# Ten column blocks of a gated MLP by one level of Strassen's scheme, with their weights fetched in three phases

## The chip, the cores and the metric

The kernel runs on one core of a Trainium2 chip. The metric is the time of one execution on the device in microseconds (us); lower is better. The engines are TensorE (PE for its matmuls, PEld for its weight loads), VectorE (DVE), ScalarE (ACT), GpSimd (POOL) and SyncE (SP, whose queue issues nearly all DMAs).

## What is computed

Attention over 4 batches, 8 heads, 768 tokens and 64 features per head, masked to pairs of tokens in the same hash bucket, and then a gated MLP on its output `x` (3072 tokens by 512), cut from the reference:

```python
scores = scale * np.matmul(q, k.transpose(0, 1, 3, 2))
scores = np.where(mask, scores, -1000000000.0)
attn = softmax(scores)                       # max taken off, exp, divided by the sum
x = np.matmul(attn, v)                       # laid out as 3072 tokens x 512
gate = 1.0 / (1.0 + np.exp(-(x @ w_gate)))   # 512 x 1536, float64 weights
val = x @ w_val                              # 512 x 1536
out = (gate * val @ w_out).astype(np.float32)  # 1536 x 512
```

## The kernel before

**Numbers.** Every product of the MLP is made of three matmuls: both operands are split in a high and a low part in fp32r, and low x high, high x low and high x high are added in PSUM. The weights come as 64-bit floats and are turned into 32-bit ones on DVE, ACT and POOL ("conversion": `exponent`, `shifted`, `mantissa`, `whole`, `signed`, `scaled` in `load_w`), and then split (`high`, `low`).

**Tiles.** The 1536 hidden columns are 12 blocks `j` of 128. Tokens go in units `(b, g)`: batch `b` (4), half `g` (2) of its 768 tokens, so a unit has 384. For one unit and one block, gate and value take 4 chunks of 128 input features x 3 matmuls each (`product`, L438: 24 matmuls of 384 columns), and the output takes 3 token tiles x 3 matmuls of 512 columns (`out_product`, L471: 9). I call these 33 matmuls one column. There are 96 columns.

**Stages.** The attention stage walks through 16 pairs of heads (6 score steps each, 96 in all). In it the weights of blocks `j` 0 to 9 are converted, one per 2.2 score steps from step 12 on (`W_KEY`, `W_STEP`), and those of blocks 3 to 9 are written to DRAM (`kept`). The first `J1` = 3 blocks of the first six units are computed there too (`moe_early`), and their part of the output is written to DRAM (`part`): 18 columns. When attention has ended (`switch`), its memory is given to the other weights, and `moe_late` does the rest unit by unit: all 12 blocks for the last two units, 9 for the other six, 78 columns. Blocks 10 and 11 are converted at its beginning. Here DVE multiplies the value in PSUM by the gate (`gated`, L454), ACT makes the high part, and POOL mostly the low one (L459).

**Order.** All instructions are tasks of a planner (`Plan`): each has an engine (or two to choose from), a cost, tasks it follows, and buffers that it takes and gives. The planner plays this through with its own costs and writes the fixed order of every engine's queue. An engine waits at the head of its queue; nothing overtakes.

Of the kernel before, what the change touches and what calls it, by code (L numbers as in the profile page):

```python
# [169 lines left out]
def lsh_attention_glu_kernel(ctx, tc, q, k, v, proj, w_gate, w_val, w_out, out):  # L170
# [137 lines left out]
    def load_w(key, n, j, early, last=None):  # L308
# [21 lines left out]
        def exponent():  # L330
            z["ex"] = stage().tile([P, N_EL], I32, name=f"ex{n}{j}", tag="wex", bufs=2 if last else 1)
            nc.vector.tensor_scalar(z["ex"], z["high"], 0x7FF00000, None, op0=ALU.bitwise_and)
# [4 lines left out]
        def mantissa():  # L337
            z["mf"] = stage().tile([P, N_EL], I32, name=f"mf{n}{j}", tag="wmf", bufs=2 if last else 1)
            nc.vector.tensor_scalar(
                z["mf"], z["high"], 0x000FFFFF, 0x00100000, op0=ALU.bitwise_and, op1=ALU.bitwise_or  # L340
            )
# [14 lines left out]
        def high():  # L356
            if early or last:
                z["w"] = (w1 if early else stage()).tile([P, 2, N_EL], F32R, name=f"w{n}{j}", tag=f"w{n}{j}")
                weights[n, j] = z["w"][:, 0], z["w"][:, 1]
            else:  # L360
                z["w"] = stage1.tile([P, 2, N_EL], F32R, name=f"w{n}{j}", tag="wk", bufs=stock["wk"])
            nc.scalar.copy(z["w"][:, 0], f(z["ex"]))

        def low(eng):
            eng.tensor_sub(z["w"][:, 1], f(z["ex"]), f(z["w"][:, 0]))

        def keep():
            nc.sync.dma_start(kept[n, j], f(z["w"]))

        def fetch():  # L370
            w = later["w"].tile([P, 2, N_EL], F32R, name=f"w{n}{j}", tag=f"w{n}{j}")
            weights[n, j] = w[:, 0], w[:, 1]
            nc.sync.dma_start(f(w), kept[n, j])

        a = dma(key, CROWDED if last and j == J2 else 524288, load, after=[last or score_tasks[min(int(key), 90)]], take=["raw2" if last else "raw1"])
        b1 = add(key, "dve", 440, exponent, after=[a], take=["mid2" if last else "mid1"])
# [3 lines left out]
        d = add(key, "dve", 700, signed, after=[b2, c2], give=["raw2" if last else "raw1"])  # L380
        e = add(key, "pool", 1300, lambda: scaled(nc.gpsimd), after=[d])
        h = add(key, "act", 560, high, after=[e], take=[] if early or last else ["wk"])
        made[n, j] = add(key, "pool", 1300, lambda: low(nc.gpsimd), after=[h], give=["mid2" if last else "mid1"])
        if not early and not last:
            a = dma(key, 524288, keep, after=[made[n, j]], give=["wk"])
            fetches.append(((n, j), a, fetch))
# [6 lines left out]
    in_turn = dict(x=[], ob=[])  # L393

    def load_x(u, b, g, stored):
        z = {}

        def load():
            z["xr"] = xp.tile([P, KC, GN], F32, name=f"xr{u}", tag="xr")
            cols = slice(g * GN, (g + 1) * GN)  # L400
            nc.sync.dma_start(z["xr"], xd[b][:, :, cols].rearrange("c p t -> p c t"))

        def high(c):
            if c == 0:
# [3 lines left out]
            nc.scalar.copy(z["xh"][:, c], z["xr"][:, c])

        def low(c, eng):  # L410
            eng.tensor_sub(z["xl"][:, c], z["xr"][:, c], f(z["xh"][:, c]))
# [15 lines left out]
    def product(key, u, n, j, x, prev, last, late=False, pace=None):  # L427

        z = {"bank": ["z"] if late else ["moe", "one"]}

        def part(c):
            if c == 0:
                pool, tag = (later["ps"], "z") if late else (ps, "one")
                z["acc"] = pool.tile([P, 512], F32, name=f"z{n}{j}_{u}", tag=tag)
            hi, lo = weights[n, j]
            wc = slice(c * P, (c + 1) * P)
            for i, (a, xx) in enumerate(((lo, "xh"), (hi, "xl"), (hi, "xh"))):
                nc.tensor.matmul(  # L438
                    z["acc"][:, :GN], a[:, wc], x[xx][:, c, :],
# [508 lines left out]
```

## Time and profile before

| | |
|---|---|
| time of three runs, us | 1077.53, 1076.45, 1075.06; median 1076.45 |
| profiled execution: first to last instruction | 1071.9 us |
| PE busy | 1048.6 us (98%) |
| DVE, ACT, POOL busy | 552.2, 491.8, 260.9 us |
| chain that ended last | PE 81%, DVE 7%, ACT 4%, POOL 3% |
| HBM read, written | 70.78 MB, 28.84 MB |

The time of the profiled execution outside its span isn't listed; the median of the runs lies 4.55 us above the span. Matmul spans in the profile overlap, since they are pipelined, so the pace of PE is read from starts, not from durations. "L438" is line 438 of the kernel before.

### The profile page before, as it was taken

The page shows a single profiled execution, that of the slowest core. Times are in us where ns is not written, and L with a number is a line of the kernel's source. Part 1 is how long each engine was busy: PE and PEld are TensorE (multiplying, and loading weights), DVE is VectorE, ACT ScalarE, POOL GpSimd, SP SyncE. Part 2 cuts the span into 40 slices and gives each one's busy share as a digit, 9 for nine tenths or more (in the row PEclk, how much of TensorE's full clock was granted, in tenths as well). Part 3 has the DMA queues.
Part 4 walks back from the last instruction along what each step waited for, and adds up shares of the span by engine and source line. Part 5 has one row for each costly group of instructions (what it writes and reads, how often), then busy time and mean ns, then how long its engine had stood idle before and what let it go on. Part 6 is the DMA issues. An engine that isn't in the chain of part 4 may idle for free.

```text
span 1071.9 us, 20499 instructions
## 1 busy us (share of the span) xinstructions
PE 1048.6 (98%) x8409; PEld 849.0 (79%) x8412; DVE 552.2 (52%) x1170; ACT 491.8 (46%) x890; POOL 260.9 (24%) x239
## 2 busy tenths in 40 slices
PE   8999999999999999999999999999999999999998
PEld 5666667677676677676668999999999999999997
DVE  5888889988888878768741261111020202120201
ACT  1868786858677676657652232122121212121211
POOL 0003233332424232311003262122121212121211
PEclk9999999999999999999999999999999999999999
DMA  8146464564756554732118511002020202020000
GB/s 206 48 118 162 132 191 128 166 195 132 220 181 186 168 165 132 235 93 67 56 61 334 204 60 60 1 1 89 1 89 1 89 1 89 1 89 1 31 30 30
DMA packets 110846, 113.54 MB, mean 106 GB/s; under 512 B 60320, under 2 KB 92064, under 8 KB 110752
## 3 DMA queue, kind: packets, MB, share of 16 engines
q1 hardware_dynamic: 109024, 111.83, 34.1%
q8 instruction: 66, 1.08, 0.4%
q10 hardware_dynamic: 1728, 0.40, 0.2%
q14 instruction: 28, 0.23, 0.1%
HBM read 70.78 MB, written 28.84 MB: 93 GB/s over the span
## 4 chain that ended last, share of the span: by engine, by line
PE 81%; DVE 7%; ACT 4%; POOL 3%; DMA 2%; issue 2%; SPq 0%; POOLq 0%; DVEq 0%; ACTq 0%
PE pv L819 10%; PE zv_0l L438 8%; PE zv_1l L438 7%; PE sc L740 7%; PE zg_0l L438 7%; PE zg_1l L438 7%; PE yo_0l L471 7%; PE yo_1l L471 7%; PE tp L802 5%; PE zg L438 3%; PE zv L438 3%; PE zo L471 3%; PE sc L734 3%; DVE e L750 2%; ACT e L769 2%
## 5 line engine op out<-in xcount | busy, mean ns | idle before, releaser
L769 ACT ACTIVATE e<-e,st 128x768 f32<-128x768 f32 x192 | 196.5, 1025 | 71.1 <-DVE st L762 70.7
L750 DVE TENSOR_SCALAR_CACHE_REDUCE e<-sc 128x768 f32<-128x768 f32 x192 | 177.8, 951 | 23.2 <-PE sc L740 22.3
L819 PE MATMUL pv<-ef,vr 128*64 128x384 f32 x768 | 141.2, 498 | 0.0
L454 DVE TENSOR_TENSOR gf_1l<-zv_1l,sig 128x384 f32<-128x384 f32 x39 | 21.8, 558 | 208.5 <-PE zv_1l L438 208.5
L454 DVE TENSOR_TENSOR gf_0l<-zv_0l,sig 128x384 f32<-128x384 f32 x39 | 21.7, 558 | 192.5 <-PE zv_0l L438 192.5
L802 PEld LDWEIGHTS tp<-ident,e 64*128 64x128 f32 x2304 | 85.2, 139 | 38.9 <-issue 16.3
L802 PE MATMUL tp<-ident,e 64*128 64x64 f32 x2304 | 97.5, 226 | 5.3 <-ACT ef L809 2.9
L809 DVE COPY ef<-tp 128x768 f32<-128x768 f32 x87 | 82.0, 950 | 34.8 <-PE tp L802 32.5
L819 PEld LDWEIGHTS pv<-ef,vr 128*64 128x64 f32 x768 | 48.5, 137 | 54.5 <-issue 49.5
L740 PE MATMUL sc<-kh,ql 64*128 64x384 f32 x192 | 90.3, 470 | 0.0
L740 PE MATMUL sc<-kh,qsl 64*128 64x384 f32 x192 | 90.3, 470 | 0.0
L809 ACT COPY ef<-tp 128x768 f32<-128x768 f32 x105 | 81.6, 791 | 11.5 <-PE tp L802 11.1
L438 PE MATMUL zg_0l<-xh_0l,wg 128*128 128x384 f32 x312 | 86.5, 337 | 0.0
L438 PE MATMUL zg_1l<-xh_1l,wg 128*128 128x384 f32 x312 | 86.4, 337 | 0.0
L438 PE MATMUL zv_0l<-xh_0l,wv 128*128 128x384 f32 x312 | 85.5, 334 | 0.0
L438 PE MATMUL zv_1l<-xh_1l,wv 128*128 128x384 f32 x312 | 85.5, 334 | 0.0
L459 POOL TENSOR_TENSOR gl<-gf_1l,gh 128x384 fp32r<-128x384 f32 x39 | 40.5, 1039 | 184.4 <-ACT gh L458 184.4
L829 POOL TENSOR_TENSOR xs<-xs,rb 128x384 f32<-128x384 f32 x32 | 33.2, 1039 | 199.9 <-ACT xs L826 126.9
L459 POOL TENSOR_TENSOR gl<-gf_0l,gh 128x384 fp32r<-128x384 f32 x37 | 39.2, 1059 | 155.8 <-ACT gh L458 155.7
L734 PE MATMUL sc<-kb,qb 64*128 64x384 bf16 x384 | 64.9, 331 | 9.4 <-ACT ef L809 3.3
L471 PE MATMUL yo_0l<-wo,gh 128*128 128x512 f32 x234 | 73.5, 395 | 0.0
L471 PE MATMUL yo_1l<-wo,gh 128*128 128x512 f32 x234 | 73.5, 395 | 0.0
(151 smaller groups left out, 2453.0 us busy)
## 6 DMA issues: line engine op xcount, KB each, us to landing
kr<-in_k_dram SPq DMA_DIRECT2D x64, 96.0 KB
vr<-in_v_dram SPq DMA_DIRECT2D x16, 384.0 KB
qsh<-qh SPq DMA_DIRECT2D x32, 192.0 KB
qsl<-ql SPq DMA_DIRECT2D x32, 192.0 KB
rb<-rd SPq DMA_DIRECT2D x64, 96.0 KB
xd<-xs SPq DMA_DIRECT2D x32, 192.0 KB
rawg<-in_moe_w_gate_dram SPq DMA_DIRECT2D x12, 512.0 KB
rawv<-in_moe_w_val_dram SPq DMA_DIRECT2D x12, 512.0 KB
```

The costliest lines, as they stand in the source:

```text
L438: nc.tensor.matmul(z["acc"][:, :GN], a[:, wc], x[xx][:, c, :], start=(c == 0 and i == 0), stop=(c == KC - 1 and i == 2),)
L454: nc.vector.tensor_mul(z["gf"], z["acc"][:, :GN], sig[:, j])
L459: low = lambda eng: eng.tensor_sub(gl[:, j], z["gf"], f(gh[:, j]))
L471: nc.tensor.matmul(acc, a[:, slot, ts_], w, start=(first and i == 0), stop=(last and i == 2))
L734: nc.tensor.matmul(sc[:, j, :GN], z["qb"][rows, c], z["kb"][rows, h], start=True, stop=False, tile_position=(j * D, 0),)
L740: nc.tensor.matmul(sc[:, j, :GN], q_[rows, c], z["k" + x][rows, h * GN : (h + 1) * GN], start=False, stop=(m == 2), tile_position=(j * D, 0),)
L750: nc.vector.tensor_scalar(sp(e), gz["sc", t, h][:, :, :GN], -SCALE, None, op0=ALU.mult, op1=ALU.min, accum_out=gz["st", t][:, 0, h : h + 1],)
L769: nc.scalar.activation(e, e, AF.Exp, bias=st[:, 2, h : h + 1], scale=st[:, 1, h : h + 1], accum_out=gz["su"][:, h * GT + t : h * GT + t + 1],)
L802: nc.tensor.transpose(tp[:, r, at_ : at_ + D], gz["e", t, h][rows, c * P : (c + 1) * P], ident[rows, rows], tile_position=(r * D, 0),)
L809: copy(gz["ef", c].rearrange("p (n r d) -> p r n d", r=2, d=D), gz["tp", c][:, :, :GN].rearrange("p r (n d) -> p r n d", d=D),)
L819: nc.tensor.matmul(gz["pv"][rows, :GN], z["v"][:, h, c], gz["ef", c][:, h * GN : (h + 1) * GN], start=(c == 0), stop=(c == NC - 1), tile_p ...
L829: nc.gpsimd.tensor_mul(gz["xs"], gz["xs"], gz["rb"])
```

## The change

`J1` goes from 3 to 2, so that 16 columns are done in the old way (`moe_early` now for all eight units, the last two of them after attention), and the other ten blocks go by Strassen's scheme (Winograd's form: 7 block products, 15 sums).

**Blocks.** Two hidden blocks make a set (`SETS`: (2,3) to (10,11)), two units of one batch a pair. The 2x2 blocks are: of `x`, unit by half of the 512 features; of a weight, half of the features by hidden block. Each of 7 products (`group`, `STEPS`, in the order 1, 2, 5, 6, 3, 7, 4) is 2 chunks x 3 matmuls of 384 columns, so gate or value of a set takes 42 matmuls for a pair, where 48 stood before.

**Sums of weights.** `combined` converts the two weights of a set and makes B12-B11, B22-(B12-B11), B22-B12 and so on on POOL or DVE before they are split and kept in DRAM (`t1` to `t4`). The sets (2,3), (4,5), (6,7) are done in the attention stage (24 weights are converted there, where it were 30), (8,9) and (10,11) after it (12, where it were 6).

**Sums of x.** `x_pair` loads the four blocks of a pair, makes S1 to S4 (POOL or DVE, 128x768 each), and splits seven blocks (ACT high, POOL or DVE low, 128x768 each). Each block has one buffer, free when the pair's last value group has used it.

**Sums of products.** Every product has a PSUM bank of its own (six banks). ACT copies products 1 and 5 to SBUF, DVE adds six times per group from PSUM and SBUF (L758), and POOL or DVE adds once (`both`). The gate times the value is now a product of two SBUF tiles, on POOL or DVE.

**Phases.** `PHASES`: two sets, two sets, one set. In each phase all four batches go by, `x` is loaded and split anew for each pair, the weights of the phase are fetched from DRAM, and the output's part is fetched, added (DVE) and stored. In the last phase a pair's output products (`outs`) stand behind the next pair's groups.

Core of the diff (planner costs, release of buffers and lines of like kind left out):

```diff
-    J1 = 3
-    J2 = 10
+    J1 = 2
+    QUARTERS = 3
+    SETS = [(j, j + 1) for j in range(J1, NJ, 2)]
+    PHASES = [SETS[i : i + 2] for i in range(0, len(SETS), 2)]
...
+        for name in ("a11", "a21", "a22", "a12"):
+            raw(name)
+        pieces_of("a11")
+        summing("s1", "a21", "a22", ALU.add, [])
+        pieces_of("s1")
+        summing("s2", "s1", "a11", ALU.subtract, [ready["s1"]])
+        pieces_of("s2")
+        pieces_of("a12")
+        summing("s4", "a12", "s2", ALU.subtract, [ready["a12"]])
+        pieces_of("s4")
+        summing("s3", "a11", "a21", ALU.subtract, [got["s1"]])
+        pieces_of("s3")
+        pieces_of("a22")
...
+        1: ("a11", 0, 0), 2: ("a12", 0, 1), 5: ("s1", 1, 0), 6: ("s2", 1, 1), 3: ("s4", 3, 0), 7: ("s3", 2, 0), 4: ("a22", 2, 1),
...
+            block, piece, half = STEPS[m]
+            hi, lo = pieces[js, n, piece]
+            for c in range(2):
+                wc = slice(half * HF + c * P, half * HF + (c + 1) * P)
+                for i, (a, xx) in enumerate(((lo, "h"), (hi, "l"), (hi, "h"))):
+                    nc.tensor.matmul(
+                        bank[m], a[:, wc], x[xx, block][:, c, :], start=(c == 0 and i == 0), stop=(c == 1 and i == 2),
+                    )
...
+        for m in (1, 2, 5, 6, 3, 7, 4):
+            prev = pe(m)
+            if m == 1:
+                snap(1, "m1")
+            elif m == 2:
+                plus(2, "m1", (0, 0), tag=tag)
+                finish((0, 0))
+            elif m == 5:
+                snap(5, "t")
+            elif m == 6:
+                plus(6, "m1", "u", after=[told[0, 0]], tag="sn")
...
+            elif m == 3:
+                plus(3, "t", (1, 0), tag=tag)
+                finish((1, 0))
+            elif m == 7:
+                plus(7, "t", (1, 1), give=["sn"], tag=tag, after=[told[1, 0]])
+                finish((1, 1))
+                plus(7, "u", "u", after=[told[1, 1]])
+            elif m == 4:
+                plus(4, "u", (0, 1), give=["z", "sn"], tag=tag)
+                finish((0, 1))
```

**What moves on DVE.** After attention, DVE's queue before holds the conversion of late weights, with one PSUM multiply per column between (`raw`, `mf`, `ex` are a weight's tiles, `gf` the gated value):

```order
L344 SCALAR_TENSOR_TENSOR mfo_9357<-rawo_9259,mfo_9357 128x512
L454 TENSOR_TENSOR gf_3_0l<-zv_3_0l,sig 128x384
L349 SCALAR_TENSOR_TENSOR exo_9351<-rawo_9259,exo_9351 128x512
L459 TENSOR_TENSOR gl<-gf_3_0l,gh 128x384
L332 TENSOR_SCALAR exv_9395<-rawv_9346 128x512
L339 TENSOR_SCALAR mfv_9406<-rawv_9346 128x512
```

Now, in the first pair of the first phase (`sn`, `sg`, `gf`: sums of products; `a12`, `s1`, `sc`, `ra`: blocks of the next pair's x; `yo`: output):

```order
L650 TENSOR_TENSOR a12l_1_9342<-ra_1_9030,a12h_1_9328 128x768
L758 TENSOR_TENSOR snuv_0_0_9357<-z6v_0_0_9335,snm1v_0_0_9310 128x384
L364 SCALAR_TENSOR_TENSOR exg_9312<-rawg_9255,exg_9312 128x512
L650 TENSOR_TENSOR s1l_1_9370<-sc_1_9151,s1h_1_9359 128x768
L758 TENSOR_TENSOR gf(1, 0)v_0_0_9384<-z3v_0_0_9347,sntv_0_0_9354 128x384
L642 TENSOR_TENSOR sc_1_9151<-sc_1_9151,ra_1_8962 128x768
L772 TENSOR_TENSOR gf(1, 0)v_0_0_9384<-gf(1, 0)v_0_0_9384,sg(1, 0)g_0_0_9287 128x384
L758 TENSOR_TENSOR gf(1, 1)v_0_0_9410<-z7v_0_0_9362,sntv_0_0_9354 128x384
L642 TENSOR_TENSOR ra_1_9030<-ra_1_9030,sc_1_9151 128x768
L789 TENSOR_TENSOR gl(1, 0)4_0_0_9413<-gf(1, 0)v_0_0_9384,gh(1, 0)4_0_0_9412 128x384
```

Between two adds that empty PSUM banks (L758) now stand a late weight's conversion (L364), the next pair's sums and low parts (L642, L650), and the multiply and low part that the output product waits for (L772, L789).

**What moves on PE.** Before, the output products stand between the last value product of one unit and the first gate product of the next:

```order
L438 MATMUL zv_3_0l<-xl_0l,wv_9440 128x384
L438 MATMUL zv_3_0l<-xh_0l,wv_9440 128x384
L471 MATMUL yo_3_0l<-wo_9393,gl 128x512
L471 MATMUL yo_3_0l<-wo_9393,gh 128x512 x2
L471 MATMUL yo_3_0l<-wo_9393,gl 128x512
L471 MATMUL yo_3_0l<-wo_9393,gh 128x512 x2
L471 MATMUL yo_3_0l<-wo_9393,gl 128x512
L471 MATMUL yo_3_0l<-wo_9393,gh 128x512 x2
L438 MATMUL zg_3_1l<-xh_1l,wg_1416 128x384
```

Now, at the first pair's end in the last phase (`z4v_2_0` is product 4 of the value, phase 2, batch 0):

```order
L733 MATMUL z4v_2_0_13057<-a22h_0_12777,wv_10_12613 128x384 x2
L733 MATMUL z4v_2_0_13057<-a22l_0_12796,wv_10_12613 128x384
L733 MATMUL z4v_2_0_13057<-a22h_0_12777,wv_10_12613 128x384
L733 MATMUL z1g_2_1_13069<-a11h_1_13014,wg_10_12478 128x384
L733 MATMUL z1g_2_1_13069<-a11l_1_13028,wg_10_12478 128x384
```

At this one boundary nothing stands between the last use of one pair's x blocks and the first of the next pair's; at the others it is 36 or 72 output products.

**What moves on POOL.** Before, POOL's queue after attention is low parts, about one per column:

```order
L459 TENSOR_TENSOR gl<-gf_3_0l,gh 128x384
L411 TENSOR_TENSOR xl_1l<-xr_1l,xh_1l 128x384
L459 TENSOR_TENSOR gl<-gf_3_0l,gh 128x384
L411 TENSOR_TENSOR xl_1l<-xr_1l,xh_1l 128x384
L459 TENSOR_TENSOR gl<-gf_3_1l,gh 128x384 x11
```

Now, at the same boundary as on PE above:

```order
L642 TENSOR_TENSOR sc_1_12855<-sc_1_12855,ra_1_12798 128x768
L650 TENSOR_TENSOR a22l_1_13095<-ra_1_12814,a22h_1_13076 128x768
L772 TENSOR_TENSOR gf(1, 1)v_2_0_13092<-gf(1, 1)v_2_0_13092,sg(1, 1)g_2_0_12984 128x384
L650 TENSOR_TENSOR s2l_1_13122<-sc_1_12855,s2h_1_13107 128x768
L789 TENSOR_TENSOR gl(0, 1)10_2_0_13142<-gf(0, 1)v_2_0_13120,gh(0, 1)10_2_0_13141 128x384
```

The low part of `a22`, whose buffer is the last to come free, stands ahead of that of `s2`, which PE takes fourth.

More of the change, by code (lines that the diff above doesn't have):

```diff
@@ L306, in lsh_attention_glu_kernel, with converted @@
     fetches = []
-    def load_w(key, n, j, early, last=None):
+    def converted(key, n, j, late, which, after, first):
         z = {}
-        stage = lambda: later["w"] if last else stage1
+        stage = lambda: later["w"] if late else stage1
+        raw_, token = ("raw2", "cv2") if late else ("raw1", "cv1")
         def load():
-            z["raw"] = raw = stage().tile([P, 2 * N_EL], I32, name=f"raw{n}{j}", tag="wraw", bufs=2 if last else 1)
+            z["raw"] = raw = stage().tile([P, 2 * N_EL], I32, name=f"raw{n}{j}", tag="wraw")
             if n == "o":
@@ L354, in scaled @@
             eng.tensor_mul(f(z["ex"]), f(z["mf"]), f(z["ex"]))
[L356 to L376, printed above, removed]
+        a = dma(key, 524288, load, after=after + last_load[late], take=[raw_])
+        last_load[late] = [a]
+        b1 = add(key, "dve", 440, exponent, after=[a], take=[token] if first else [])
         b2 = add(key, "act", 700, shifted, after=[b1])
@@ L379, in load_w @@
         c2 = add(key, "dve", 700, whole, after=[c1])
[L380 to L386, printed above, removed]
+        d = add(key, "dve", 700, signed, after=[b2, c2], give=[raw_])
@@ new lines, in converted, with split, high, low @@
+        return z, add(key, "pool", 1300, lambda: scaled(nc.gpsimd), after=[d])
+    def split(key, src, to, size, late, after, give, tile_of=None):
+        z = {}
+        wk = "wk2" if late else "wk1"
+        def high():
+            if tile_of is not None:
+                z["w"] = tile_of()
+            else:
+                stage = later["w"] if late else stage1
+                z["w"] = stage.tile([P, 2, size], F32R, name=f"p{to.name}", tag="wk", bufs=stock[wk])
+            nc.scalar.copy(z["w"][:, 0], src())
+        def low():
+            nc.gpsimd.tensor_sub(z["w"][:, 1], src(), f(z["w"][:, 0]))
+        part_ = size / N_EL
+        h = add(key, "act", 60 + 500 * part_, high, after=after, take=[wk] if tile_of is None else [])
+        low_ = add(key, "pool", 100 + 1200 * part_, low, after=[h], give=give)
+        if tile_of is not None:
+            return low_, low_
+        return low_, dma(key, 1024 * size, lambda: nc.sync.dma_start(to, f(z["w"])), after=[low_], give=[wk])
@@ L871, in group @@
             )
-        a = add(n - 6, either(summed), after=[prev], take=["xs"], give=["one"])
+        ends = i == len(heads) - 1 and g == NG - 1
+        a = add(n - 6, either(summed), after=[prev], take=["xs"], give=["one"] + ["moe"] * ends)
         a = add(n - 4, "pool", 1230, divided, after=[a, spread_], give=["rb"])
```

435 lines of the change are left out of this document (333 added, 102 removed).

## The prediction

> **What bounds the kernel now.** I read the page first (busy shares, the chain that ended last), then windows by stage, then the timeline inside the end stage.
>
> ```profile
> span 1071.9 us, 20499 instructions
> PE 1048.6 (98%) x8409; PEld 849.0 (79%) x8412; DVE 552.2 (52%) x1170; ACT 491.8 (46%) x890; POOL 260.9 (24%) x239
> PE 81%; DVE 7%; ACT 4%; POOL 3%; DMA 2%; issue 2%; SPq 0%; POOLq 0%; DVEq 0%; ACTq 0%
> ```
>
> PE carries the chain. The windows (columns: span, busy us and instruction count of PE, PEld, DVE, ACT, POOL, granted clock, DMA share, GB/s) show two stages. In attention all engines are loaded; after 576 us PE alone is.
>
> ```profile
> 8.00:120.00 112.00, 106.40 (x1208) 70.01 (x1209) 95.52 (x231) 76.68 (x135) 16.62 (x14) 1.00 0.51 128
> 120.00:360.00 240.00, 232.35 (x2444) 167.25 (x2444) 209.97 (x451) 175.38 (x309) 81.28 (x69) 0.99 0.58 174
> 576.00:1068.00 492.00, 490.57 (x2562) 454.94 (x2560) 91.72 (x135) 99.96 (x202) 112.59 (x102) 1.00 0.16 57
> ```
>
> PE's pace is read from starts:
>
> ```profile
> 1051.06 0.56 DVE L454 TENSOR_TENSOR gf_1l<-zv_1l,sig 128x384 f32<-128x384 f32 x1 [5.71 <-PE zv_1l L438]
> 1054.95 0.33 PE L438 MATMUL zv_1l<-xh_1l,wv 128*128 128x384 f32 x1
> 1057.03 0.39 PE L471 MATMUL yo_1l<-wo,gl 128*128 128x512 f32 x1
> 1057.32 0.56 DVE L454 TENSOR_TENSOR gf_1l<-zv_1l,sig 128x384 f32<-128x384 f32 x1 [5.71 <-PE zv_1l L438]
> 1059.11 0.33 PE L438 MATMUL zg_1l<-xh_1l,wg 128*128 128x384 f32 x1
> ```
>
> Twelve value matmuls take 2.08 us (0.173 each), nine output matmuls 2.08 (0.231 each); a column comes round in 6.26 us, the sum of 24 and 9 of them. 78 columns x 6.26 = 488 us: the end stage is PE at its pace, with no waits to speak of.
>
> **Term 1, matmuls removed.** Ten blocks are five sets, times two (gate, value), times four pairs, times 6 matmuls fewer: 240 x 0.173 = **-41.6 us**. The pace stays: same shapes, a fresh weight load per matmul as before. Output matmuls keep their number.
>
> **Term 2, the attention stage.** Six columns (37.6 us) leave it and return after it; that nets to nothing only if attention shrinks by as much. The same three windows restricted to the bf16 score matmuls (L734, 24 per pair of heads), the early gate and value matmuls (L438) and the early output matmuls (L471):
>
> ```profile
> 8.00:120.00 112.00, 16.18 (x96) 5.82 (x96) 1.00 0.51 128
> 120.00:360.00 240.00, 26.45 (x156) 8.70 (x156) 0.99 0.58 174
> 360.00:540.00 180.00, 22.17 (x132) 7.22 (x132) 1.00 0.41 125
> 120.00:360.00 240.00, 42.47 (x216) 36.74 (x216) 0.99 0.58 174
> 360.00:540.00 180.00, 28.34 (x144) 24.52 (x144) 1.00 0.41 125
> 120.00:360.00 240.00, 18.68 (x72) 12.89 (x72) 0.99 0.58 174
> 360.00:540.00 180.00, 16.55 (x63) 11.27 (x63) 1.00 0.41 125
> ```
>
> Without early columns a pair costs 112/4 = 28.0 us. From 120 to 360 us, less 216 x 0.173 + 72 x 0.231 = 54.0 us, (240 - 54.0)/6.5 = 28.6. So early columns simply add up, and taking six out should give 37.6 us back. From 360 to 540 us, with conversion mostly over, the same reckoning gives 25.5. Conversion now ends 13 score steps (2.2 pairs) earlier, 24 weights instead of 30 at the same pace: at most 2.2 x 3.1 = -7 us. Against it, half-width sums on POOL and more copies on DVE, while DVE is 87% busy already (209.97 of 240): up to +8. I take **-2** (nearer the first, since six conversions leave too).
>
> **Term 3, the change of stage.** PE now has 25 us of work behind attention's last product (6 output groups, 96 gate and value matmuls of the last two units) while x and the first weights come. Up to the end of the first set's gate weights some 4.6 MB are in the queue (x of the last unit 0.8, of the first pair 1.6, output parts 0.5, weights 1.75), with its value and output weights 7.4 MB. The DMA rate there:
>
> ```profile
> 576.00:600.00 24.00, 24.00 (x131) 22.82 (x130) 2.23 (x4) 4.54 (x9) 4.04 (x4) 1.00 1.03 405
> ```
>
> At 405 GB/s that is 11 and 18 us, inside the cover; the second set's weights follow when the early weights' space is free, with about 10 us before PE wants them. If that cover falls short PE waits up to about 10. The last unit's x must still go out and back through DRAM: **+3** (0 to 10).
>
> **Term 4, DVE and POOL after attention.** PE per pair and two sets: 168 x 0.173 + 72 x 0.231 = 45.7 us. DVE's and POOL's durations:
>
> ```profile
> 607.84 0.42 DVE L332 TENSOR_SCALAR exg<-rawg 128x512 int32<-128x512 int32 x1
> 608.17 0.42 DVE L339 TENSOR_SCALAR mfg<-rawg 128x512 int32<-128x512 int32 x1
> 613.63 0.56 DVE L454 TENSOR_TENSOR gf_0l<-zv_0l,sig 128x384 f32<-128x384 f32 x1 [2.35 <-PE zv_0l L438]
> 614.11 0.68 DVE L344 SCALAR_TENSOR_TENSOR mfv<-rawv,mfv 128x512 f32<-128x512 uint32 x1
> 614.77 0.56 DVE L459 TENSOR_TENSOR gl<-gf_0l,gh 128x384 fp32r<-128x384 f32 x1
> 611.36 1.29 POOL L354 TENSOR_TENSOR exg<-mfg,exg 128x512 f32<-128x512 f32 x1 [1.56 <-DVE exg L349]
> 645.46 1.02 POOL L411 TENSOR_TENSOR xl_1l<-xr_1l,xh_1l 128x384 fp32r<-128x384 f32 x1 [3.67 <-ACT xh_1l L408]
> 645.83 2.36 DVE L411 TENSOR_TENSOR xl_1l<-xr_1l,xh_1l 128x384 fp32r<-128x384 f32 x2 [0.31 <-ACT xh_1l L408]
> 646.43 1.34 POOL L459 TENSOR_TENSOR gl<-gf_0l,gh 128x384 fp32r<-128x384 f32 x1
> 619.00:641.00 22.00, 22.00 (x116) 20.43 (x115) 17.32 (x21) 8.17 (x15) 15.19 (x12) 1.00 0.15 48
> ```
>
> An add from PSUM occupies DVE 0.48 us (start to start). Two DVE operations with both inputs in SBUF took 2.36 us beside POOL, 1.18 each, and POOL's 1.02 became 1.34: they exclude each other. From 619 to 641 us POOL was busy 69% and DVE 17.32 us, of which four PSUM multiplies are 1.9; its 17 other operations, at the free spacings above (0.33 for eight, 0.66 for eight, 0.48 for one), make 8.4, so they were stretched about 1.85 times. PE lost nothing there.
>
> Phase 0, by the built order, has on POOL 116 us over four pairs (1.02 per 384, 1.29 per 512, 1.85 per 768 by the step between these two), 63% of PE's 183. DVE per pair: 24 adds (11.5), 6 output adds (3.7), and 17.2 us of SBUF operations and conversion, stretched by as much: 47 in all against PE's 45.7. So DVE just doesn't keep up: 4 x 1.3 = 5, and 3 more since a queue in fixed order can't run full. **+8** (0, as in the window above, to 44 if each of some 38 operations per pair pays the row's 0.64 and DVE sets the pace at 57).
>
> Phase 1 has no conversion: DVE 30 of 45.7, hidden by six banks' slack. **+2** (0 to 8) for the chain add, multiply, high, low that the output product waits for behind 768-wide operations.
>
> Phase 2 has 22.9 us of PE per pair, with a full x preparation in each. DVE sums to 78 of 91.5. The boundary without output products between: `a22` is free when PE ends the value group; then ACT 0.9, POOL 1.85, 1.02 and 1.85 for `s2`: 5.7 us after, where PE wants `s2` 3 steps x 1.04 = 3.1 after. That is a sure 2.7, and some for the other two. **+6** (2.7 to 20).
>
> **Term 5, the clock after a wait.** One place shows what a wait costs beyond itself:
>
> ```profile
> 124.10 0.43 DVE L332 TENSOR_SCALAR exv<-rawv 128x512 int32<-128x512 int32 x1 [2.15 <-DMA rawv<-in_moe_w_val_dram]
> 127.11 0.34 PE L734 MATMUL sc<-kb,qb 64*128 64x384 bf16 x2 [1.66 <-DVE ef L809]
> 128.85 0.52 PE L740 MATMUL sc<-kl,qsh 64*128 64x384 f32 x1
> 128.00:132.00 4.00, 4.00 (x26) 2.09 (x24) 2.96 (x8) 0.54 (x2) 1.28 (x1) 0.66 0.77 194
> ```
>
> DVE stood 2.15 us at a weight that hadn't landed, PE then idled 1.66, and the granted clock was 0.66 for 4 us, which lost about 1.4 more. Conversion stands in DVE's queue in phase 0 in the same way. Two such events: **+3** (0 to 8). The Trainium skill (TensorE: Matmul & The Clock Gate, Part 1) has the clock halve only after an idle window of about 3.4 us; by that rule waits of 1 to 3 us cost only themselves and the sum would be 3 lower. This trace, with 1.66 us, speaks against relying on it.
>
> **Sum.** -41.6 - 2 + 3 + 8 + 2 + 6 + 3 = -21.6: span 1050.3. The runs' median lies 4.55 us above the profiled span (1076.45 against 1071.9), which I keep: **1055 us**.
>
> ACT isn't a term: per pair 24 operations of 384 at 0.5 us and seven of 768 at 0.93 (two of 384 took that), 18.5 of 45.7 us.
>
> ```profile
> 645.70 0.51 ACT L458 CAST gh<-gf_0l 128x384 fp32r<-128x384 f32 x1
> 644.86 0.93 ACT L408 CAST xh_1l<-xr_1l 128x384 fp32r<-128x384 f32 x2 [1.59 <-PE zv_0l L438]
> ```
> DMA isn't one either: per pair about 1.6 MB of x and 3.1 MB of output parts, at the 405 GB/s above 12 us of 45.7, of 22.9 in phase 2.
>
> **Rivals.**
> *The cover holds* (13%). If waits stay as small as in the window 619 to 641, only the sure 2.7 and a few more are left: 1071.9 - 41.6 + 3 to 13, or 1038 to 1048 with the 4.55. For it: PE at 22.00 of 22 under a busier POOL. Against: six banks are 6 us of slack, and waits come in chains.
> *DVE and POOL set the pace* (12%, two thirds of it still below 1074). Term 4's ends instead of its middle: +44, +8 and +20, at the most 1071.9 - 41.6 - 2 + 3 + 72 + 3 = 1106, +4.55 = 1111; half of the excess gives about 1083. It is slower than before from 41.6 us of waits on, 3.5 per pair over twelve pairs. Against: the stretch of 1.85 is measured under a busier POOL than phase 0 will have. The Trainium skill (SBUF — State Buffer, Who interferes with whom) lets a second two-input operation block fully until the first is done, but exempts those with at most one SBUF input, as the 240 product adds are; the trace agrees: such multiplies took 558 ns in the mean over the whole end stage.
>
> ```profile
> L454 DVE TENSOR_TENSOR gf_0l<-zv_0l,sig 128x384 f32<-128x384 f32 x39 | 21.7, 558 | 192.5 <-PE zv_0l L438 192.5
> ```
>
> *Attention doesn't shrink* (8%). If DVE and ACT, not PE, set its pace, as in 8 to 120 us at 28.0 per pair without early columns, half of the 37.6 us stays: about 1055 + 19 = 1074, no change that a run can tell. Against: 28.0 and 28.6 with and without columns.
>
> **Chances.** My forecast (1043 to 1067 by the terms' middles) has 67%, the rivals 13, 12 and 8. A run can tell a change of about 0.2%, 2.2 us. Slower: a third of the second rival and a third of the third, 7%; within: 4%; faster: 89%. The range 1037 to 1074 leaves out the best of the first rival and the slow ends of the other two.
>
> **What would show it.** Attention's last product stands here:
>
> ```profile
> 560.89 1.51 PE L819 MATMUL pv<-ef,vr 128*64 128x384 f32 x8
> ```
>
> Right: it ends near 523 us (562 before), POOL near 60% and DVE near 90% busy in the 185 to 195 us of phase 0, PE near its pace in phase 1, one wait of 3 us or so at the first boundary of phase 2, granted clock at 1.00 but for a few stretches. Wrong: PE waiting on L758, L789 or L650 in every pair, clock below 0.95 in a phase, or attention ending after 540 us.

## The result: 4.8% slower, and the profile after

The changed kernel takes 1126.45 us (median of 4 runs, 1125.4 to 1130.04) against 1075.93 for the kernel before: ratio 1.0477, 95% interval 1.0456 to 1.0498. The forecast was 1055, range 1037 to 1074. The profiled execution has a span of 1123.3 us, 51.4 more than before. Its page (span, busy times, granted clock by slice, chain that ended last):

```profile
span 1123.3 us, 21291 instructions
...
PE 1033.1 (92%) x8172; PEld 822.5 (73%) x8172; DVE 877.5 (78%) x1568; ACT 577.2 (51%) x1035; POOL 463.5 (41%) x358
...
PEclk9999999999999999999999999898989998998899
...
PE 53%; DVE 26%; issue 8%; DMA 5%; ACT 5%; POOL 3%; SPq 0%; DVEq 0%; POOLq 0%; ACTq 0%
```

PE carried 81% of the chain before, now 53%; DVE's share went from 7% to 26%, and the clock dips in the late stage. Windows by stage (attention, change of stage, phases 0, 1, 2; columns as in the prediction):

```profile
8.00:542.30 534.30, 512.75 (x5609) 351.94 (x5607) 458.09 (x1011) 368.49 (x653) 146.81 (x137) 1.00 0.51 150
542.30:574.31 32.01, 28.14 (x133) 24.37 (x133) 13.10 (x13) 14.46 (x27) 18.19 (x12) 0.95 0.82 295
...
574.31:794.31 220.00, 196.16 (x979) 178.14 (x979) 183.71 (x243) 86.81 (x160) 138.78 (x95) 0.95 0.61 213
794.31:1004.88 210.57, 191.07 (x962) 175.88 (x960) 138.12 (x181) 68.12 (x127) 102.66 (x70) 0.95 0.38 129
1004.88:1123.30 118.42, 99.33 (x481) 89.99 (x479) 83.25 (x110) 39.34 (x69) 55.39 (x34) 0.93 0.40 137
```

PE's work at the paces of the prediction (0.173 and 0.231 us) is some 182.9 us in phases 0 and 1 each (phase 0 has 4.2 of early output products besides) and 91.4 in phase 2. Over that lie **32.9, 27.7 and 27.0 us** (the last with the tail of some 4.6), and 7.1 in the change of stage (24.9 of work): 95 us in all behind attention. In the kernel before it was 13 (509.5 us for 1896 x 0.173 + 729 x 0.231 = 496.4). So the 51.4 us are -41.6 of matmuls, +82 behind attention and +11 in attention, which lost 31.1 us of PE's work and got only 20.1 shorter.

The waits of PE behind attention (total, times, longest):

```profile
PE yo L855 <- DVE ol L893: 12.3, 6, 3.9
PE yo L855 <- DVE gl(1, 0)4_0_2_10424 L789: 6.7, 1, 6.7
...
PE yo L855 <- DVE gl(1, 0)8_1_0_11437 L789: 4.9, 1, 4.9
PE yo L855 <- DVE gl(1, 0)8_1_3_12794 L789: 4.9, 1, 4.9
...
PE z6g L733 <- ACT s2h L646: 3.9, 1, 3.9
```

Inside a pair the gate and value groups run at PE's pace (14.59 us from one set's first product to the next's). The loss stands at the pair's boundary: the output products wait for the low part `gl` of (1,0), and further on for the output adds `ol`, which free their PSUM banks. One such boundary of phase 1 in time order, DVE first, then POOL, then PE:

```profile
877.27 0.55 DVE L758 TENSOR_TENSOR gf(1, 0)v<-z3v,sntv 128x384 f32<-128x384 f32 x1
877.74 2.35 DVE L650 TENSOR_TENSOR s3l<-ra,s3h 128x768 fp32r<-128x768 f32 x1
880.00 2.15 DVE L772 TENSOR_TENSOR gf(1, 0)v<-gf(1, 0)v,sg(1, 0)g 128x384 f32<-128x384 f32 x1
882.08 0.55 DVE L758 TENSOR_TENSOR gf(1, 1)v<-z7v,sntv 128x384 f32<-128x384 f32 x1
...
883.41 1.35 DVE L789 TENSOR_TENSOR gl(1, 0)8_1_1_11884<-gf(1, 0)v,gh(1, 0)8_1_1_11883 128x384 fp32r<-128x384 f32 x1
```

```profile
877.42 1.84 POOL L642 TENSOR_TENSOR sc<-sc,ra 128x768 f32<-128x768 f32 x1 [1.83 <-DVE s1l L650]
879.23 2.51 POOL L650 TENSOR_TENSOR a22l<-ra,a22h 128x768 fp32r<-128x768 f32 x1
```

```profile
884.81 0.80 PE L855 MATMUL yo<-wo,gl(1, 0)8_1_1_11884 128*128 128x512 f32 x1 [4.87 <-DVE gl(1, 0)8_1_1_11884 L789]
```

DVE's low piece of 128x768 takes 2.35 us, ending 0.8 after POOL's sum; the multiply behind it takes 2.15 and ends 0.4 after POOL's `a22l`. The adds from PSUM (L758) keep 0.55 beside all this. Two readings were possible: the place of the next pair's `x` in DVE's queue, or POOL as a neighbour.

### The profile page after: what moved, and what is told of

It is laid out like the page before. It is cut to its first block, busy times and chain, and to the rows that moved or that the text cites. A ratio compares the mean times of both kernels' runs of the same rounds, so it can differ in the third digit from the quotient of the medians.

```text
span 1123.3 us, 21291 instructions
## 1 busy us (share of the span) xinstructions
PE 1033.1 (92%) x8172; PEld 822.5 (73%) x8172; DVE 877.5 (78%) x1568; ACT 577.2 (51%) x1035; POOL 463.5 (41%) x358
## 4 chain that ended last, share of the span: by engine, by line
PE 53%; DVE 26%; issue 8%; DMA 5%; ACT 5%; POOL 3%; SPq 0%; DVEq 0%; POOLq 0%; ACTq 0%
PE yo L855 10%; PE pv L1136 8%; PE sc L1057 6%; PE tp L1119 4%; DVE e L1067 4%; PE sc L1051 3%; PE zv L517 2%; PE zo L550 2%; DVE ef L1126 2%; ACT e L1086 2%; PE zg L517 2%; DVE gf(1, 0)v L772 2%; PE z6g L733 1%; PE idle L289 1%; DMA rawg<-in_moe_w_gate_dram 1%
## 5 line engine op out<-in xcount | busy, mean ns | idle before, releaser
L1126 DVE COPY ef<-tp 128x768 f32<-128x768 f32 x100 | 94.2, 950 | 23.1 <-PE tp L1119 23.0
L1136 PEld LDWEIGHTS pv<-ef,vr 128*64 128x64 f32 x768 | 47.6, 136 | 53.5 <-issue 46.3
L1057 PE MATMUL sc<-kh,qsh 64*128 64x384 f32 x192 | 64.6, 337 | 0.0
L1057 PE MATMUL sc<-kh,qh 64*128 64x384 f32 x192 | 64.6, 336 | 0.0
L1057 PE MATMUL sc<-kl,qh 64*128 64x384 f32 x192 | 64.3, 335 | 0.0
L1057 PE MATMUL sc<-kl,qsh 64*128 64x384 f32 x192 | 64.3, 335 | 0.0
L1051 PEld LDWEIGHTS <-qb 64*128 64x128 bf16 x384 | 22.8, 95 | 50.4 <-issue 45.4
L893 DVE TENSOR_TENSOR ob<-yo,ob 128x512 f32<-128x512 f32 x36 | 24.7, 686 | 29.1 <-PE yo L855 26.8
L808 POOL TENSOR_TENSOR sntg<-sntg,snug 128x384 f32<-128x384 f32 x16 | 18.4, 1153 | 67.5 <-DVE snug L758 67.5
L893 DVE TENSOR_TENSOR ol<-yo,ol 128x512 f32<-128x512 f32 x36 | 24.6, 684 | 21.3 <-PE yo L855 18.1
L855 PE MATMUL yo<-wo,gh 128*128 128x512 f32 x120 | 40.0, 417 | 0.0
```

Source lines behind the costliest of these rows:

```text
L855: nc.tensor.matmul(accs[t], a[:, ts_], w, start=(slot == 0 and jj == 0 and q == 0), stop=(slot == len(sets) - 1 and jj == 1 and q == 2),)
L893: FIRST, "dve", 640, lambda: nc.vector.tensor_add(z["ob"], accs[t], z["ob"]), after=[prev, a],
L1051: nc.tensor.matmul(sc[:, j, :GN], z["qb"][rows, c], z["kb"][rows, h], start=True, stop=False, tile_position=(j * D, 0),)
L1057: nc.tensor.matmul(sc[:, j, :GN], q_[rows, c], z["k" + x][rows, h * GN : (h + 1) * GN], start=False, stop=(m == 2), tile_position=(j * D, 0),)
L1126: copy(gz["ef", c].rearrange("p (n r d) -> p r n d", r=2, d=D), gz["tp", c][:, :, :GN].rearrange("p r (n d) -> p r n d", d=D),)
L1136: nc.tensor.matmul(gz["pv"][rows, :GN], z["v"][:, h, c], gz["ef", c][:, h * GN : (h + 1) * GN], start=(c == 0), stop=(c == NC - 1), tile_p ...
```

## Experiments

Ratios are to the kernel before, run on the same chip; times are medians. Unless a base is named, the edit is made in the changed kernel. The diffs are shortened, and some of their lines say in words what the edit does.

**1. Hold (e1).** The next pair's `x` behind the chain:

```diff
+ summing/pieces_of (phases 0, 1): after += previous pair's sigs[-1]["h", (0, 0)], ["h", (1, 0)]
```

> The sums and low pieces of the next pair's x (phases 0 and 1) wait until the highs and lows of the last value group's first two halves, (0,0) and (1,0), are done; nothing else is moved. Theory A, order in DVE's queue: in the changed kernel these 768-wide operations stand between the product add and the multiply and low that the output products wait for (2.35 us and more of them ahead of gl in phase 1). Then the wait of 4.9 us in each pair of phase 1 falls under 2, the pairs go from 52.2-53.2 us to about 47, phase 0 wins some 10 to 15 of its 33 us, and the time falls by 25 to 40, to 1087-1100 us. Theory B, too much work on DVE and POOL whatever its order: the wait moves to the next pair's first s1 and s2 products, the pairs keep their length within 1 us, and the time stays within 6 us of 1126.

Measured: 1127.83 us, ratio 1.0481 (1.0448 to 1.0514). Unchanged: phase 0 is 5 us shorter (214.7), phase 1 4 longer (214.5). In phase 1 one pair of four still shows the 4.9 us wait for `gl`, and the rest moved, behind attention, to the output adds:

```profile
PE yo L857 <- DVE ol L895: 36.3, 11, 6.5
PE yo L857 <- DVE gl(1, 0)8_1_3_12794 L790: 4.9, 1, 4.9
```

The time is theory B's, but the wait went to the output adds and not to the next pair's first products. This change of order is worth nothing: what is pushed back from one place delays the next.

**2. DVE alone in phases 1 and 2 (e2).**

```diff
- [("pool", ..., ...), ("dve", ..., ...)]      # x_pair's `on`, finish's multiply and low, `both`
+ [("dve", ..., ...)]                          # where the phase is 1 or 2
```

> In phases 1 and 2 every sum, multiply and low piece stands on DVE alone; POOL has nothing there. Phase 0 stays as it is. Theory C, DVE and POOL exclude each other: the 2.15 us multiplies and 2.35 us low pieces go back to about 0.5 and 1; DVE then has 24 product adds x 0.48, six output adds x 0.62, 11 x 0.95 and 20 x 0.48 = 35 us of 45.7 per pair, which is no more than the 34 it shows now, and phase 1's pairs fall to about 47 us, phase 2 loses its 4 us at the first boundary: together -25 to -35, 1091 to 1101 us. Theory A (the order in the queue alone): eleven x operations instead of some on POOL now stand in the chain, each 0.95, so the wait stays at 3 to 5 us: within 8 us of 1126. Theory B (volume): DVE's busy time grows past 40 us per pair and the time rises.

Measured: 1096.64 us, ratio 1.02 (1.0162 to 1.0237), 30 us less than the changed kernel; the run in the profile is the fastest of the four, 1092.11. Phase 1 in its window, and two groups of DVE's instructions there (mean ns of one), then the same groups and the add from PSUM in the changed kernel:

```profile
793.24:980.72 187.48, 183.62 (x961) 170.25 (x960) 143.10 (x246) 67.42 (x126) 2.58 (x2) 1.00 0.42 139
```

```profile
L773 DVE TENSOR_TENSOR gf(1, 0)v<-gf(1, 0)v,sg(1, 0)g 128x384 f32<-128x384 f32 x8 | 4.5, 556 | 0.1
L650 DVE TENSOR_TENSOR s3l<-ra,s3h 128x768 fp32r<-128x768 f32 x4 | 3.8, 960 | 0.0
```

```profile
L650 DVE TENSOR_TENSOR s3l<-ra,s3h 128x768 fp32r<-128x768 f32 x4 | 9.4, 2348 | 0.0
L772 DVE TENSOR_TENSOR gf(1, 0)v<-gf(1, 0)v,sg(1, 0)g 128x384 f32<-128x384 f32 x4 | 8.6, 2150 | 0.0
L758 DVE TENSOR_TENSOR gf(0, 1)v<-z4v,snuv 128x384 f32<-128x384 f32 x8 | 4.4, 551 | 0.4
```

DVE has 246 instructions instead of 181 in phase 1 and is busy 143.1 us instead of 138.1: what POOL did in 100 us (102.66 less the 2.58 left) costs DVE 5, because its own are no longer stretched. Phase 1 falls from 210.6 to 187.5 us, phase 2 from 118.4 to 109.6.

**3. Fill (e3).** Work for PE ahead of each pair's output products, about as long as the wait (4.6 us):

```diff
+ for _ in range(20 if t == slot == 0 and len(sets) == 2 else 0):
+     nc.tensor.matmul(accs[t], oh[:, :P], oh, start=True, stop=True)
```

> In phases 0 and 1, 20 matmuls of 128x512 whose result is thrown away (4.6 us at full clock) stand ahead of each pair's output products, where PE waits 2.4 to 6.7 us now. Nothing is taken out of any other queue. Theory D, the clock: half of the loss of a boundary is the stretch of 3.4 or 6.8 us at half clock that follows the wait (about 50 us of such stretches in phases 0 and 1, that is some 25 us lost); with PE busy through the wait these stretches go and the time falls by 10 to 20 us in spite of 160 extra matmuls (37 us), to 1106-1116. Rival: the wait costs only itself, the clock record says nothing of the time: the time stays within 5 us, or rises by up to 10 where the waits were shorter than 4.6.

Measured: 1126.76 us, ratio 1.0481 (1.0456 to 1.0506). Phases 0 and 1, and the wait that came in the place of the one filled:

```profile
576.69:795.25 218.56, 207.64 (x1059) 188.25 (x1059) 184.51 (x243) 86.51 (x160) 140.02 (x95) 1.00 0.62 216
795.25:1005.11 209.86, 202.54 (x1041) 185.07 (x1040) 138.22 (x181) 68.25 (x127) 102.93 (x70) 1.00 0.38 128
```

```profile
PE yo L858 <- DVE ol L896: 18.1, 13, 3.9
```

The clock is 1.00 now, 160 extra matmuls are done, and the phases are as long as before (220.0 and 210.6). The stretches at half clock did follow the waits, but in these phases they cost nothing that shows: with PE at full speed it waits for the output adds instead.

**4. An eighth product put back** into every group, thrown away, in the changed kernel (e14) and in the best version (e15; its base, e12, is in part 8):

```diff
+ for _ in range(6 if m == 1 else 0):
+     nc.tensor.matmul(bank[m], hi[:, :P], x["h", block][:, 0, :], start=True, stop=True)
```

> The changed kernel with an eighth product back in every group: six more matmuls of 128x384 ahead of the first product, thrown away; 240 matmuls, 41.6 us of PE. If DVE and POOL set the length of the pairs (52.3 us in phase 1 for 45.7 of PE's work), the pairs hardly get longer until PE's work passes 52: phase 1 +1 to +8 of its 16.6, all in all +8 to +22, 1134-1148 us. Rival (PE's own work still counts fully, the waits come on top): +36 to +44, 1162-1170.

Measured: 1164.53 us, 38 more than the changed kernel: the rival. Phase 1 of it and its waits:

```profile
807.81:1036.42 228.61, 209.10 (x1057) 193.56 (x1056) 137.87 (x181) 68.52 (x127) 103.27 (x70) 0.95 0.36 118
```

```profile
PE yo L857 <- DVE gl(1, 0)8_1_3_12986 L791: 4.9, 1, 4.9
PE yo L857 <- DVE gl(1, 0)8_1_0_11557 L791: 4.9, 1, 4.9
```

Phase 1 grew by 18.0 us for 16.6 of matmuls, and the wait is 4.9 us as before. So DVE and POOL are not short of time over the pair (DVE is busy 66% of phase 1). They are short of it at the boundary: only when the last value group has used a block of `x` is its buffer free, so the next pair's sums and low pieces, that group's add, multiply, high and low, and six output adds all fall within the 16.6 us of output products. A burst of fixed length, whatever PE does before it, fits this run and e3 alike.

> The same eighth product put back into the version on DVE alone with the new keys. There phases 0 and 1 run within 2% of PE's pace, so by the theory the 240 matmuls cost 34 to 42 us (a few hide in phase 2's boundaries): 1096 to 1106 us. Rival: less than 25, which would mean that PE isn't what bounds that version either.

Measured: 1099.94 us, 37.7 more than the same version without it. In both kernels the products are worth 38 of the 41.6 us.

**5. POOL as a neighbour only (e10).** To e2, work on POOL that nobody waits for:

```diff
+ if u[0] == "1" and m in (2, 6, 7):
+     add(FIRST, "pool", 2000, lambda: nc.gpsimd.tensor_sub(sig, sig, sig), after=[done[m]])
```

> The kernel with phases 1 and 2 on DVE alone (1096.6 us; phase 1 187.5 us), and in phase 1 twelve subtractions of 128x768 per pair on POOL for which nobody waits (on a tile that nothing reads any more), about 22 us of POOL per pair, as in the changed kernel (24.9). Theory C, exclusion: DVE's operations with both inputs in SBUF are stretched again from 0.95 to 2 and more, and phase 1's pairs go from 46.6 to between 49 and 53 us: phase 1 198 to 212 us, the time up by 10 to 24. Rival, POOL was slow as a member of the chain and not as a neighbour: phase 1 stays at 187 to 190.

Measured: 1126.15 us, ratio 1.045 (1.0424 to 1.0476), 29.5 more than without; phase 1 took 214 us instead of 187.5. With nothing to wait for, the 48 subtractions ran through one after the other and were over in the second pair, so that one run shows both cases. Part of POOL's queue, then the first pair's second part and the third pair, and a low piece of the first pair (count, total us, mean ns):

```profile
814.64 55.29 POOL L747 TENSOR_TENSOR sig<-sig 128x768 f32<-128x768 f32 x30
```

```profile
840.00:869.02 29.02, 18.01 (x57) 13.71 (x58) 26.71 (x23) 3.20 (x5) 27.84 (x16) 0.71 0.31 103
...
921.19:967.82 46.63, 45.84 (x241) 42.58 (x240) 35.52 (x61) 16.54 (x31) 0.00 (x0) 1.00 0.31 104
```

```profile
L650 DVE TENSOR_TENSOR s3l<-ra,s3h 128x768 fp32r<-128x768 f32 x1 | 2.2, 2220 | 0.0
```

The pairs last 68.6, 52.2, 46.6 and 46.6 us (47.7 for the first in e2). With POOL busy, 23 DVE instructions take 26.7 us; without, 61 take 35.5 (another mix), and the low piece that takes 960 ns in e2 takes 2220. The work of DVE and PE is e2's, so POOL as a neighbour alone can make a loss of this size, 26.5 us in phase 1, more than the 10 to 24 expected. It worked here without a break for one and a half pairs; in the changed kernel 100 us of it are spread over four, so how much of the 23 us there comes from POOL's own place in the chain isn't separated.

**6. DVE alone everywhere, and where the weights are converted.**

```diff
  # run e5: all phases on DVE for x, multiplies, low pieces, sums of products
  # runs e7 and e6: e5, and
- QUARTERS = 3
+ QUARTERS = 4 (run e7), 5 (run e6); a phase's weights are fetched after those of the phase before
```

> As the run with x, sums, multiplies and low pieces on DVE alone in phases 1 and 2, and now in phase 0 too; on POOL there is left only the conversion of the last two sets. Theory C (exclusion of DVE and POOL): phase 0 took 220 us against 183 of PE's work, its DVE then has 35 us per pair and 6 of conversion, and POOL's own 1.3 to 1.9 us operations collide some 30 times instead of some 70: phase 0 falls by 12 to 25 us, the time to 1072-1085 (1096.6 in the run before it). Rival: phase 0 is bound by the landing and conversion of weights (the chain of waits shows DMA of rawg and rawv there): it stays within 5 us of 218.

> As the run with everything on DVE in all phases, and the fourth set's weights are converted and combined in attention too, one set stays for phase 0. By theory C phase 0 falls by another half of what conversion costs there, 5 to 10 us; attention pays 3 to 5 us for the set (three sets cost it 11 beyond the early columns that left). Net -1 to -6. If attention is already full (DVE 92 to 94% busy from 120 to 360 us), the set costs as much as it brings: 0 to +5.

> As before it, with all five sets converted and combined in attention, nothing in the phases. Phase 0 then has the same work as phase 1: by theory C it takes 186 to 190 us, as phase 1 did with DVE alone (187.5); POOL is idle after attention and no DVE operation with both inputs in SBUF takes over 1.2 us there. Attention ends 6 to 12 us later than 542. Net against the run with all on DVE: -5 to -20. Rival (conversion is not what holds phase 0): phase 0 stays above 200 us and the net is a loss.

Measured: 1078.41, 1074.51 and 1076.21 us; ratios 1.0026 (1.001 to 1.0043), 0.9988 (0.9968 to 1.0008), 1.0008 (0.9986 to 1.003). Phase 0 of the three, in the same order (profiled runs of 1078.42, 1076.84 and 1080.6 us):

```profile
568.22:773.12 204.90, 197.74 (x1021) 181.75 (x1021) 168.54 (x289) 85.90 (x158) 39.39 (x32) 0.99 0.63 220
```

```profile
576.74:777.90 201.16, 195.68 (x1021) 180.87 (x1021) 161.06 (x275) 82.61 (x152) 27.49 (x23) 1.00 0.62 210
```

```profile
589.09:781.98 192.89, 188.45 (x979) 173.54 (x979) 143.56 (x246) 69.78 (x130) 1.53 (x2) 1.00 0.50 168
```

The first two have 42 output products more in that window (1021 for 979, 9.7 us). Over PE's work phase 0 loses 8.1, 4.4 and 5.8 us instead of 32.9: `x` and the chain off POOL did it; conversion on POOL beside it matters little in phase 0 (the last set's tail made phase 1's first pair 53.5 us in e5). In e6 phase 0 takes 192.9 us, not the 186 to 190 expected. The fourth and fifth set put off attention's end by 8.3 and 6.5 us (its last product starts at 541.6, 549.9 and 556.4), which eats most of what the fourth brings and all that the fifth does.

**7. Attention.** The kernel before with two columns early; the changed kernel without combining; another pace; the sums on DVE:

```diff
- J1 = 3                      # kernel before
+ J1 = 2
```

> The kernel before with one number changed: two column blocks instead of three ride in attention, the other ten (conversion in attention as before, 30 weights) are computed after it; nothing of Strassen's scheme. 6 of 18 early columns leave attention (37.6 us of PE's time, of which some 10 stood behind its end before). Theory E, attention is held by DVE and not by PE once a column is gone: its last product ends at 545 to 552 instead of 562, and the time rises by 12 to 20 us, to 1088-1096. Rival, the reckoning of the prediction (columns add up): it ends at 528 to 534 and the time stays within 4 us of 1076.

```diff
- todo = [(0, ...), (3, ...), (1, t12), (2, t34)]
+ todo = [(0, za), (1, zb)]   # in attention; t1 to t4 left out
```

> The changed kernel without the combination of weights in attention: of each of the first three sets, the two weights are converted and split as they are; the four half-width sums and the split of one and a half further pieces are left out, and the phases read pieces of the plain weights in their place (so the numbers of these sets are not those of the scheme; all products and transfers of the phases stay). Theory F, the combinations are what attention lost: its last product ends at 529 to 534 instead of 542. Theory E (DVE full of conversions, fewer columns give nothing back): the end moves by less than 4 us. The stage behind keeps its length of 581 us within 3 us in both, so the time is 1110-1117 or 1122-1127.

Measured: 1082.01 (ratio 1.0051, 1.0032 to 1.007) and 1121.26 us (1.0415, 1.039 to 1.0439). Attention's last product in the changed kernel, in the kernel before with two columns, and without combining (the last four of the eight matmuls):

```profile
540.78 1.51 PE L1136 MATMUL pv<-ef,vr 128*64 128x384 f32 x8
```

```profile
535.71 1.51 PE L819 MATMUL pv<-ef,vr 128*64 128x384 f32 x8
```

```profile
535.76 0.81 PE L1144 MATMUL pv<-ef,vr 128*64 128x384 f32 x4
```

And the early products within attention, before (L438, L471) and with two columns:

```profile
0.00:562.40 562.40, 80.30 (x409) 69.47 (x409) 1.00 0.50 145
...
0.00:562.40 562.40, 35.23 (x135) 24.16 (x135) 1.00 0.50 145
```

```profile
0.00:537.22 537.22, 56.78 (x288) 48.97 (x288) 1.00 0.54 155
...
0.00:537.22 537.22, 24.88 (x91) 15.80 (x91) 1.00 0.54 155
```

121 x 0.173 + 44 x 0.231 = 31.1 us of work left, and the kernel before got 25.2 shorter there: columns add up to 81%, between the two expectations; what holds the other 5.9 us isn't shown. Without combining, attention ends at 536.6 with 24 conversions, at 537.2 with 30 of the kernel before: six conversions fewer gave 0.6 us, not 7. Combining costs 5.7 (542.3 for 536.6), theory F's direction, but only half of the loss. (Behind attention this run lost 4.5 us that nothing here explains.)

```diff
- W_KEY, W_STEP = 12.0, 2.2
+ W_KEY, W_STEP = 12.0, 2.75   # run e4
  # run e8: t1 to t4 on DVE alone in attention
```

> One number: the weights' conversions in attention are started 2.75 score steps apart instead of 2.2, so that 24 weights take as long as 30 did before. Theory E, density: DVE is 92 to 94% busy in 120 to 360 us because 24 conversions and the six combinations of weights come at the old pace; spread out, DVE falls under 90% there, PE's waits at the exponent and turn chains shrink and attention's last product ends at 532 to 537 instead of 542; the time falls by 5 to 10 us, the end stage unchanged. Rival: attention has about 11 us of extra work on DVE, ACT and POOL wherever it is put: the end stays within 2 us of 542 and the time within 3 us of 1126.

> The changed kernel with one thing moved: the four half-width sums of each combination of weights stand on DVE alone in attention, not on POOL when it is free; phases untouched. Theory C for attention: POOL's 24 sums of 0.65 to 1.3 us stretch DVE's two-input operations, so off POOL attention ends 2 to 5 us earlier than 542 although DVE has 8 us more of work. Theory E (DVE is simply full): attention ends 3 to 8 us later. The end stage keeps its length within 2 us in both.

Measured: 1123.99 us (1.046, 1.043 to 1.0491), attention's last product at 537.3, 3.5 us earlier; and 1129.54 us (1.0506, 1.0466 to 1.0546), at 541.0, unchanged. Spreading helps a little; which engine makes the sums does not show in attention. The 3 us that the latter lost lie behind it and stay open.

**8. A better version.** On e7: conversions 2.4 steps apart, and another order on DVE in phase 2:

```diff
- FIRST                                   # multiply, high, low of gated values in phase 2
+ FIRST + 1                               # run e11: behind all of x
+ FIRST + b + 1.5, x of pair b: FIRST + b # run e12: x of b+1, values of b, x of b+2
```

> The version with four sets converted in attention and all of the phases on DVE (1074.5 us), with two numbers changed: in phase 2 multiplies and low pieces of the gated values come behind the next pair's x in DVE's order (their products are a pair away), and conversions come 2.4 steps apart instead of 2.2. Phase 2 took 110.6 us there against 91.4 of PE's work and 4.5 of the tail; its first boundary 30.75 of 22.9. Expected: first boundary to 24-26, the others 1 to 2 less each, together -5 to -10; attention -1 to -4; 1061 to 1069 us, 1% faster than the kernel before. Rival (x's chain itself, not the place in the queue, is what PE waits for): phase 2 falls by less than 3 us, and the time stays at 1070-1074.

> The version of 1070.6 us with another order on DVE in phase 2 alone: x of the next pair first, then multiplies and low pieces of this pair's gated values, then x of the pair after it. In the run before, x of two pairs ahead stood before the low pieces and PE waited 9.0 us for one. If the place in DVE's queue holds phase 2, the first boundary (35.0 us from z1g to z1g, 22.9 of work) falls to 24-28, phase 2 from 109 to 100-104 and the time to 1061-1066. Rival (the chain sum, high, low of x itself): boundary at 28 to 31, phase 2 at 106 or more, the time 1067-1071.

> As the run with new keys in phase 2, conversions 2.6 steps apart instead of 2.4. Theory E (density): attention's last product ends 2 to 4 us earlier than 542.6 and the time falls as much. Rival (spread far enough already): within 2 us; and if the last set's weights come too late for the change of stage, the first products of phase 0 wait and the time rises by up to 5.

Measured: 1070.57 (ratio 0.9947, 0.9927 to 0.9966), **1062.23 (0.9875, 0.9853 to 0.9897)** and 1062.77 us (0.9877, 0.9852 to 0.9902). In e11 attention ended 7 us earlier, but phase 2's first boundary got longer, as `x` of two pairs ahead went before the low pieces:

```profile
971.47:1006.47 35.00, 25.55 (x122) 22.56 (x121) 32.77 (x53) 14.57 (x24) 0.00 (x0) 0.85 0.43 143
```

```profile
PE yo L857 <- DVE gl(0, 1)10_2_0_13312 L791: 9.0, 1, 9.0
```

In e12 this boundary takes 24.61 us, near the 22.9 of work:

```profile
972.18:996.79 24.61, 23.25 (x121) 21.21 (x121) 24.39 (x42) 11.38 (x19) 0.00 (x0) 1.00 0.35 114
```

```profile
span 1058.5 us, 21195 instructions
...
PE 1011.8 (96%) x8172; PEld 807.1 (76%) x8172; DVE 865.2 (82%) x1720; ACT 583.1 (55%) x1047; POOL 208.1 (20%) x194
```

Once the stretch is gone, the order in the queue does decide. A wider pace (2.6) brings nothing more. This version is 1.2% faster than the kernel before, with the products of the changed kernel.

## Why the prediction was wrong

The forecast was 2% faster, the result is 4.8% slower: the span is 73.0 us above the forecast 1050.3. Term 4 alone lies 67.0 us above its middle values, term 2 lies 13 above. (The 13 us that the kernel before lost behind attention are not taken off in this list.)

- **Term 1, -41.6: right but for some 4 us.** An eighth product put back costs 38.1 us in the changed kernel and 37.7 in e12.
- **Term 2, attention, -2: measured +11.** The step "early columns simply add up" took 28.0 and 28.6 us per pair of heads as proof. Removing columns returns 25.2 of 31.1 us, six conversions fewer return 0.6 where the term allowed up to 7, combining costs 5.7. DVE and POOL are more, not less, busy there; the term's own range ended at +8.
- **Term 3, change of stage, +3 (0 to 10):** 7.1 us over PE's work, inside its range.
- **Term 4 is where it failed.** Phase 0, +8 (0 to 44): 32.9. Phase 1, +2 (0 to 8): 27.7. Phase 2, +6 (2.7 to 20): 22 without the tail. Phase 0 lies inside its wide range, the others outside. The volumes were about right: DVE was busy 45.9 us per pair in phase 0 for the 47 of the sum, and 34.5 in phase 1 for 30. The step that failed is the one from there to the loss. "DVE just doesn't keep up" by 1.3 us per pair, and "DVE 30 of 45.7, hidden by six banks' slack", compare sums over a pair, where the work that PE waits for comes in a burst against 16.6 us. And the stretch by 1.85 is an average of 17 operations. The pair that took 2.36 us beside POOL was read as 1.18 each; what the rows show is a wait for the end of a POOL instruction, and POOL's got twice as wide in this change, so that in the chain a low piece went from 0.95 to 2.35 and a multiply from 0.55 to 2.15. The chain add, multiply, high, low was named as phase 1's risk and then given 2 us. In phase 2 DVE alone gave back 8.8 us (118.4 to 109.6, e2), and the new order on DVE another 9.7 (110.6 in e7, 100.9 in e12).
- **Term 5, the clock, +3:** there were far more waits than two. In the phases the profile shows half clock after each wait of 3.4 us or more, and none after those of 2.4, 2.0 and 1.6 us in phase 0. But e3 shows that in phases 0 and 1 the stretches took no time that DVE would not have taken. One boundary:

```profile
880.70:884.80 4.10, 0.00 (x0) 0.00 (x0) 4.10 (x5) 2.50 (x4) 2.98 (x3) 0.95 0.81 270
884.80:888.20 3.40, 3.39 (x9) 2.67 (x9) 3.40 (x4) 0.09 (x1) 2.04 (x2) 0.56 0.06 22
```

  After the 4.87 us wait the clock is 0.56. The Trainium skill (TensorE: Matmul & The Clock Gate, Part 1) halves it after an idle window of about 3.4 us, which agrees here. The 1.66 us wait of the kernel before, with 0.66 behind it, does not agree.

- **The rival "DVE and POOL set the pace" (12%)** had the direction and the place, and its +44 and +20 reach phase 0's 32.9 and nearly phase 2's 22; its +8 for phase 1 is far below the 27.7, and its far end of 1111 us is below the result. Its mechanism as told, a pace, is not it: e14 shows none. Against it the prediction held that the stretch had been measured under a busier POOL than phase 0's. POOL's share is no measure: phase 1 lost 27.7 us with POOL 49% busy, the window before lost nothing at 69%. That the length of the instruction that DVE finds running is the measure rests on the rows above; no run varies it alone.
- Of the signs named as "wrong", PE waits on L789 in every pair of phases 0 and 1, on L650 in phase 2, attention ending after 540 us and a clock under 0.95 in phase 2 (0.93) came.

## To carry to other kernels

Two engines that exclude each other for much of their work are little more than one: before work is shared between DVE and POOL, ask what each DVE instruction with both inputs in SBUF would wait for; here DVE alone did the same work in 5 us more of its own time and 23 us less of the phase's. Compare an engine's work with the window in which its inputs and its reader allow it, not with the stage. And when an engine waits at a boundary, put work back or fill the wait: if the time follows the work and the wait stays as it was, the wait is a fixed length; if the time stays, the work was hidden.

## What the hardware showed

An instruction of DVE with two inputs in SBUF took 0.95 us (128x768) alone and 2.35 beside POOL; the add with one input in PSUM took 0.55 in both. The Trainium skill (SBUF — State Buffer, Who interferes with whom) says just that: of such an instruction and one of POOL that reads SBUF the second blocks until the first is done, and an instruction with at most one SBUF input does not contend. These rows agree with both halves. The excess in them, 1.4 us for the low piece and 1.6 for the multiply, is most of the POOL instruction beside it (1.84 and 2.51); that size is what the prediction lacked.
